# Windowed attention and a squared-relu feed-forward layer: the second chunk's steps run beside the first's, all in three products of split halves, with relu, square, scaling and splitting for two steps at once

## The chip, the cores and the metric

The kernel runs on one core of a Trainium2 chip. The metric is the device time of one execution in microseconds (us). The core's engines are TensorE (PE in the profile; PEld is its load of stationary operands), VectorE (DVE), ScalarE (ACT), GpSimd (POOL) and SyncE (SP), which issues all of this kernel's DMAs.

## The reference, cut to what matters

B, H, S, D = 4, 8, 768, 64; the feed-forward layer has 512 inputs, 2048 hidden units and 512 outputs. All is float32.

```
k_sum = k.reshape(B, H, 24, 32, D).max(axis=3)
v_sum = v.reshape(B, H, 24, 32, D).mean(axis=3)
scores_l = scale * q @ k.T, kept where |i - j| < 16, else -1e9
scores_s = scale * q @ k_sum.T + log(32)
a = softmax(concat[scores_l, scores_s])
x = a @ concat[v, v_sum]                  # 3072 tokens x 512
h = x @ w_in                              # 512 x 2048
g = s * relu(h)**2 + b
out = g @ w_out                           # 2048 x 512
```

## The kernel before, in words

The 3072 tokens are worked on in 12 chunks of 256 (three for each batch entry), the heads in four pairs p. The hidden layer is cut into 16 slices of 128 units, the steps f. For a chunk c the kernel makes x (attention) and then, for each step, the hidden layer (`hidden`, tile ph, 128 units x 256 tokens), relu and square (`activate`, tile r), scaling (`scaled`, tile g) and the projection (`project`), which adds all steps into two tiles po of 128 tokens x 512.

*Attention.* For a pair: `scores` (tile ps, L310 and L313), `masked` on VectorE (L328, tile pr), `exps` on ScalarE (L341), `normalize` on VectorE (L348, L349, L351), `transposes` on TensorE (L360, tile pt), `turned` (a copy, pT), `values` (tile pav, L394 and L396), `attended` (x, tile xh) and `attended_low` (its lower half, xl, L412). `k_max` makes block maxima of k (L165), `fill_k` and `fill_v` put maxima and means into the loaded tiles on GpSimd (L267, L272). The first chunk makes its products with maxima and means apart (`scores_of_maxima`, `mean_of_rows`, `values_of_means`).

*Weights and halves.* Weights come as 64-bit numbers in two words and are loaded by 32 DMAs (`load_weights`), scaled on ScalarE (L131, L132), and put together on VectorE (L140, L141, tile wf). A product of float32 accuracy is made in one of two ways. Plain: one fp32 product with wf. Split: wf is divided into an upper half wh (`upper_weights`, a cast to fp32r on either engine, L228 or L230) and a lower half wl (`lower_weights`, VectorE, L153), x into xh and xl, g into gh and gl (`upper_rows`, `lower_rows`, L483), and three fp32r products are added: lower by upper, upper by lower, upper by upper (L446 and L498).

*Which steps are plain.* The first chunk's steps 0 to 7 are plain (L429, and L498 with wf); its steps 8 to 15 (the table THREE) and all steps of the other chunks are split. The first chunk's x is kept whole and split later, in one piece (`first_upper`, `first_lower`, L421). The second chunk goes through the steps in another order, 8 to 15 first (SECOND). Relu, square, scaling and the split of g are one instruction for each step, 128 x 256.

*Storage.* SBUF: eight slots of 128 x 2048 hold raw weights, pairs of wh, and at the start k, q and rows of v; a ring of 17 holds wf and wl. PSUM has eight banks: two each for po, ph and ps, one for pt and one for pav.

*Order.* The program is recorded in a fixed order. From the start through most of the second chunk and the third chunk's attention it is a table written out by hand, FIRST_ORDER: a letter names a function (S scores, M masked, E exps, N normalize, T transposes, C turned, V values, X attended, y attended_low, H and Y hidden, J activate, G scaled, a and b upper and lower rows, P project, h and l upper and lower weights, A and D scaling and conversion of weights, i, o and w loads of weights, u and x loads of q with k and of v, W fillers), digits give chunk, pair or step, and stars choose the engine. Each engine works through its part of it in order. What is left follows from rules with steps (`then`): four hidden steps of a chunk, then the four projections of the group before, and so on. This loop begins with the third chunk's first four hidden steps.

Of the kernel before, what the change touches and what calls it, by code (L numbers as in the profile page):

```python
# [44 lines left out]
def windowed_attention_then_relu2_ffn(ctx, tc, qk, vwin, kt, vt, kq, vrow, wp, out):  # L45
# [33 lines left out]
    ones = const.tile([P, P], F32, name="ones")  # L79
    nc.vector.memset(ones, 1.0)  # L80
# [23 lines left out]

    THREE = (8, 9, 10, 11, 12, 13, 14, 15)
    SECOND = THREE + tuple(f for f in range(NF) if f not in THREE)


    def steps(c):
        return SECOND if c == 1 else tuple(range(NF))  # L110

# [31 lines left out]
    def upper_weights(f, other=False):  # L143
        j = SECOND.index(f)
# [38 lines left out]
    def v_mean(bi, g):  # L183
        if g == 0:
            vsum[bi] = p2.tile([P, H, D], F32, name="vsum", bufs=1)
        vs = p2.tile([96, D], F32, name="vmean")
# [17 lines left out]
    def keep_warm(n):  # L204

        t = ps_po.tile([P, DM], F32, name="warm", tag="po")
        for _ in range(n):
            nc.tensor.matmul(t[:, :P], ones, ones, start=True, stop=True)
# [80 lines left out]
    def scores(c, p, j):  # L289
        q, kw = qk_t[c, p]  # L290
        if j == 0:
# [5 lines left out]
            elif p == 2:  # L297
# [47 lines left out]
    def normalize(c, p):  # L345
# [7 lines left out]
    def transposes(c, p):  # L353
        pr = pr_of.pop((c, p))
        if together(c) and p % 2:
# [22 lines left out]
    def values(c, p):  # L378
# [3 lines left out]
        elif c < 2 or p % 2 == 0:  # L382
            if together(c) and p:
# [31 lines left out]
    def first_upper(other=False):  # L415
        xt["first"] = slot(F32R, "x0h")[:, 48 : 48 + NKC * T].rearrange("p (k t) -> p k t", t=T)
        copy(other, xt["first"], xt[0])

    def first_lower():
        xl["first"] = p2.tile([P, NKC, T], F32R, name="x0l", tag="xl")  # L420
        nc.vector.tensor_tensor(xl["first"], xt[0], xt["first"].bitcast(F32), ALU.subtract)  # L421


    ph_of, ph_both, r_of, gg, po = {}, {}, {}, {}, {}

    def hidden_part(f, kc):
        if kc == 0:
            ph_of[0, f] = ps_h.tile([P, 2, T], F32, name="ph", tag="ph")[:, f % 2]
        nc.tensor.matmul(  # L429
            ph_of[0, f], w_f[f][:, kc * P : (kc + 1) * P], xt[0][:, kc], start=(kc == 0), stop=(kc == NKC - 1)  # L430
        )

    def hidden(c, f):
        if c == 0 and f not in THREE:
            for kc in range(NKC):
                hidden_part(f, kc)
            return
        xh, xlow = (xt["first"], xl["first"]) if c == 0 else (xt[c], xl[c])
        if c < 2 or f % 2 == 0:
            ph_both[0] = ps_h.tile([P, 2, T], F32, name="ph", tag="ph")  # L440
        ph = ph_of[c, f] = ph_both[0][:, f % 2]
        terms = [
            (w[f], x, kc) for w, x in ((w_l, xh), (w_h, xlow), (w_h, xh)) for kc in range(NKC)
# [18 lines left out]
    def scaled(c, f, other=False):  # L462
        if c == 0 and f not in THREE:
            g = p2.tile([P, T], F32, name="g0", tag="gh", bufs=8)
        else:
            g = p2.tile([P, T], F32, name="g")
        gg[c, f] = (g,)
        r = r_of.pop((c, f))
        if other == 2:
            nc.scalar.activation(g, r, AF.Identity, bias=b_col, scale=s_col)  # L470
        else:
            (nc.vector if other else nc.gpsimd).tensor_scalar(g, r, s_col, b_col, ALU.mult, ALU.add)  # L472

    def upper_rows(c, f, other=False):
        (g,) = gg[c, f]
        gh = p2.tile([P, T], F32R, name="gh", tag="gh", bufs=8)
        copy(not other, gh, g)
        gg[c, f] = g, gh

    def lower_rows(c, f):  # L480
        g, gh = gg[c, f]
        gl = p2.tile([P, T], F32R, name="gl", bufs=7)
        nc.vector.tensor_tensor(gl, g, gh.bitcast(F32), ALU.subtract)  # L483
        gg[c, f] = gh, gl

    def project(c, f):
        if f == steps(c)[0]:
            for t in range(T // P):
                po[t] = ps_po.tile([P, DM], F32, name="po", tag="po")
        g = gg.pop((c, f))  # L490
        if c == 0 and f not in THREE:
            terms = [(g[0], w_f[f])]
        else:
            gh, gl = g
            terms = [(gl, w_h[f]), (gh, w_l[f]), (gh, w_h[f])]
        for t in range(T // P):
            for n, (a, w) in enumerate(terms):
                nc.tensor.matmul(  # L498
                    po[t], a[:, t * P : (t + 1) * P], w[:, 512:],
                    start=(f == steps(c)[0] and n == 0), stop=(f == steps(c)[-1] and n == len(terms) - 1),  # L500
                )

    def evict(c, t, other=False):
        o = stage.tile([P, DM], F32, name="o", tag="stage")
        copy(other, o, po[t])
# [35 lines left out]
    )  # L541
    def of(fn, *more):
# [8 lines left out]
        "F": mean_done, "t": fill_v, "X": attended, "y": attended_low, "Xh": first_upper, "Xl": first_lower,  # L551
# [55 lines left out]
    for j, f in enumerate(SECOND):  # L607
        then(NF - 3 + j, SPLIT, upper_weights, f)
        then(NF - 3 + j, SPLIT, lower_weights, f)
    for i in range(NF, NC * NF):  # L610
        c, j = divmod(i, NF)
        f = steps(c)[j]
# [68 lines left out]
```

## Time and profile before

| | |
|---|---|
| Time of the kernel, median of 3 runs | 630.0 us (629.89 to 630.21) |
| The profiled execution, its own time | 630.13 us |
| Its span, first to last instruction | 628.4 us |
| TensorE busy, share of the span | 616.9 us, 98% |
| VectorE busy | 324.2 us, 52% |
| ScalarE busy | 311.8 us, 50% |
| GpSimd busy | 178.4 us, 28% |
| Read from memory, written | 59.09 MB, 6.29 MB |

Engine busy times are sums over the span; the end of a matmul is modelled, so a busy TensorE is not one at its peak. Instructions of one engine overlap a little: what one costs in a row of them is the time from its start to the next one's start, shorter than its listed duration. Rows of the timeline give start, duration, engine, line, operation, output and input, shapes, and in brackets the idle time ahead with what ended it.

### The profile page before, as it was taken

To read this page: it belongs to the slowest core of one execution; us is meant where nothing else is said; L and a number is where in the kernel's file an instruction comes from. 1 tells how busy PE (TensorE), PEld (TensorE's weight loads), DVE (VectorE), ACT (ScalarE), POOL (GpSimd) and SP (SyncE) were. 2 spreads that over 40 slices of the span, in tenths; PEclk is the share of its full clock that TensorE was granted. 3 is DMA by queue.
4 is the path that set the end of the run, shared out by engine and by line. 5 is a ranking of instruction groups with operands and counts; after the bars stand their busy time and mean duration, and the time that the engine had idled before them with its cause. 6 is when DMAs were issued, how large, how long until landed. Compare 5 with 4: busy or idle time off the path is not lost.

```text
span 628.4 us, 14231 instructions
## 1 busy us (share of the span) xinstructions
PE 616.9 (98%) x5330; PEld 549.9 (88%) x5330; DVE 324.2 (52%) x1033; ACT 311.8 (50%) x927; POOL 178.4 (28%) x342
## 2 busy tenths in 40 slices
PE   6999999999999999999999999999999999999997
PEld 5766789989989998999899899998998999899896
DVE  6999989865354246345454235336435325523311
ACT  4999967463463364265245436436345336323321
POOL 3126213111611422322242321341151151232211
PEclk9999999999999999999999999999999999999999
DMA  8999413006205016103502211600620500200000
GB/s 340 414 418 417 196 47 120 4 16 198 75 14 181 2 45 223 50 19 102 167 19 101 82 43 49 226 19 0 221 65 2 181 0 20 85 1 2 35 0 34
DMA packets 26997, 66.45 MB, mean 106 GB/s; under 512 B 3824, under 2 KB 3824, under 8 KB 26928
## 3 DMA queue, kind: packets, MB, share of 16 engines
q1 hardware_dynamic: 26928, 65.54, 29.2%
q8 instruction: 42, 0.69, 0.4%
q14 instruction: 27, 0.22, 0.1%
HBM read 59.09 MB, written 6.29 MB: 104 GB/s over the span
## 4 chain that ended last, share of the span: by engine, by line
PE 87%; DMA 4%; DVE 3%; ACT 1%; issue 1%; DVEq 0%; SPq 0%; ACTq 0%
PE po L498 40%; PE ph L446 39%; PE pav L396 3%; DMA wraw<-in_wp_dram 3%; PE pt L360 3%; PE ps L310 3%; DMA qk<-in_qk_dram 1%; DVE wf L141 1%; DVE wf L140 1%; ACT wraw L131 0%; ACT wraw L132 0%; DVE wl L153 0%; DVE x0l L421 0%; DVE r L458 0%; DVE pr L328 0%
## 5 line engine op out<-in xcount | busy, mean ns | idle before, releaser
L472 POOL TENSOR_SCALAR g<-r,sb_col 128x256 f32<-128x256 f32 x180 | 113.5, 632 | 394.8 <-ACT r L460 267.0
L228 DVE CAST gh<-g 128x256 fp32r<-128x256 f32 x173 | 51.6, 299 | 244.4 <-POOL g L472 242.9
L454 ACT ACTIVATE r<-ph 128x256 f32<-128x256 f32 x186 | 70.2, 378 | 207.0 <-PE ph L446 197.7
L498 PE MATMUL po<-wh,gl 128*128 128x512 f32 x368 | 147.3, 400 | 0.9 <-DVE gl L483 0.9
L498 PE MATMUL po<-wh,gh 128*128 128x512 f32 x368 | 144.8, 393 | 0.0
L498 PE MATMUL po<-wl,gh 128*128 128x512 f32 x368 | 143.8, 391 | 0.0
L446 PE MATMUL ph<-xh,wl 128*128 128x256 f32 x704 | 109.4, 277 | 0.0
L446 PE MATMUL ph<-xl,wh 128*128 128x256 f32 x704 | 108.6, 276 | 0.0
L446 PE MATMUL ph<-xh,wh 128*128 128x256 f32 x704 | 108.5, 276 | 0.0
L483 DVE TENSOR_TENSOR gl<-g,gh 128x256 fp32r<-128x256 f32 x184 | 85.5, 466 | 32.8 <-PE po L498 16.5
L446 PEld LDWEIGHTS ph<-xh,wl 128*128 128x128 f32 x704 | 97.0, 188 | 4.4 <-issue 0.2
L446 PEld LDWEIGHTS ph<-xl,wh 128*128 128x128 f32 x704 | 93.4, 188 | 0.0
L446 PEld LDWEIGHTS ph<-xh,wh 128*128 128x128 f32 x704 | 92.9, 188 | 0.0
L341 ACT ACTIVATE pr<-pr,mn 128x120 f32<-128x120 f32 x176 | 66.9, 382 | 34.8 <-DVE mn L328 34.7
L498 PEld LDWEIGHTS po<-wh,gl 128*128 128x128 f32 x368 | 69.1, 188 | 16.2 <-DVE gl L483 2.0
L498 PEld LDWEIGHTS po<-wh,gh 128*128 128x128 f32 x368 | 69.1, 188 | 14.9
L498 PEld LDWEIGHTS po<-wl,gh 128*128 128x128 f32 x368 | 69.2, 188 | 13.5
L460 ACT ACTIVATE r<-r 128x256 f32<-128x256 f32 x183 | 76.5, 418 | 6.5 <-DVE r L456 0.8
L272 POOL COPY vw<-vsum 24x256 f32<-24x256 f32 x88 | 46.2, 553 | 19.9 <-PE po L498 10.8
L230 ACT COPY o<-po 128x512 f32<-128x512 f32 x23 | 13.5, 589 | 42.0 <-PE po L498 40.9
L341 ACT ACTIVATION_READ_ACCUMULATOR pr<-pr,mn 128x1 f32 x176 | 33.0, 187 | 0.0
L351 DVE TENSOR_TENSOR pr<-pr,rs 128x480 f32<-128x480 f32 x48 | 31.8, 661 | 1.7
(95 smaller groups left out, 556.5 us busy)
## 6 DMA issues: line engine op xcount, KB each, us to landing
wraw<-in_wp_dram SPq DMA_DIRECT2D x32, 512.0 KB
qk<-in_qk_dram SPq DMA_DIRECT2D x44, 369.0 KB
vw<-in_vwin_dram SPq DMA_DIRECT2D x48, 256.0 KB
out_dram<-o SPq DMA_DIRECT2D x24, 256.0 KB
kraw<-in_kt_dram SPq DMA_DIRECT2D x12, 384.0 KB
vraw<-in_vt_dram SPq DMA_DIRECT2D x12, 252.0 KB
kq<-in_kq_dram SPq DMA_DIRECT2D x4, 512.0 KB
vraw<-in_vt_dram SPq DMA_DIRECT2D x6, 264.0 KB
```

The source lines that it names most:

```text
L228: nc.vector.tensor_copy(out_, in_)
L272: nc.gpsimd.tensor_copy(vw_t[c, p][WIN:KR, e], vsum[bi][WIN : WIN + NB, 2 * p + e, :].unsqueeze(1).to_broadcast([NB, NSUB, D]),)
L310: nc.tensor.matmul(o, qi, kw[r, i, :], start=True, stop=True)
L341: nc.scalar.activation(pr, pr, AF.Exp, bias=mn_of[c, p][:, n : n + 1], scale=-1.0, accum_out=sm_of[c, p][:, n : n + 1])
L351: nc.vector.tensor_tensor(pr, pr, rs.unsqueeze(2).to_broadcast([P, 4, KR]), ALU.mult)
L360: nc.tensor.transpose(pt_of[c, p][:KR, n * P : (n + 1) * P], pr[:, n, :], ident)
L446: nc.tensor.matmul(ph, w[:, kc * P : (kc + 1) * P], x[:, kc], start=(n == 0), stop=(n == len(terms) - 1))
L454: nc.scalar.activation(r, ph, AF.Relu)
L460: nc.scalar.activation(r, r, AF.Square)
L472: (nc.vector if other else nc.gpsimd).tensor_scalar(g, r, s_col, b_col, ALU.mult, ALU.add)
L483: nc.vector.tensor_tensor(gl, g, gh.bitcast(F32), ALU.subtract)
L498: nc.tensor.matmul(po[t], a[:, t * P : (t + 1) * P], w[:, 512:], start=(f == steps(c)[0] and n == 0), stop=(f == steps(c)[-1] and n == len ...
```

## The change

The first chunk's plain steps go: all steps of all chunks are split. THREE, SECOND, `first_upper` and `first_lower` are removed; the first chunk's x is made as xh and xl at once, pair by pair, like the others. The table FIRST_ORDER is new: the second chunk's attention stands ahead of nearly all hidden steps, and the steps of the first and the second chunk follow each other, step by step, from step 0 on (H1.0, H1.1, H0.2, H1.2, H0.3 and so on); all weights are split as they come. The first chunk's steps 0 and 1 are made by `hidden_part` as before, in pieces of 128 inputs between the attention's parts, now with three products for each piece.

Relu, square, scaling and the two halves of g are one instruction for two steps, 128 x 512; scaling is made in place. The second chunk's output is added up in the PSUM banks of pt and pav, so both po banks are left to the first; the third chunk's transposes and values use the two banks of ps, and all its scores too. In the first chunks `normalize` adds its 1e-9 on GpSimd instead of VectorE. The fillers multiply the identity instead of a tile of ones, 12 of them instead of 9.

```
-    THREE = (8, 9, 10, 11, 12, 13, 14, 15)
-    SECOND = THREE + tuple(f for f in range(NF) if f not in THREE)
...
-            elif p == 2:
+            elif p == 2 and c > 2:
                 both = [ps_h.tile([P, 2 * T], F32, name="ps", tag="ph")[:, : 4 * KR] for _ in range(2)]
...
-        nc.vector.tensor_scalar(rs, sm_of.pop((c, p)), 1e-9, None, ALU.add)
+        (nc.gpsimd if other else nc.vector).tensor_scalar(rs, sm_of.pop((c, p)), 1e-9, None, ALU.add)
...
-        if together(c) and p % 2:
+        if c == 2:
+            pt_of[c, p] = ps_s.tile([P, 4 * P], F32, name="pt", tag="ps")
+        elif together(c) and p % 2:
...
-            if together(c) and p:
+            if c == 2:
+                o_of[c, p] = ps_s.tile([P, 2 * T], F32, name="pav", tag="ps")
+            elif together(c) and p:
...
-            xt[c] = p2.tile([P, NKC, T], F32R if c else F32, name="xh", tag="xh")
+            xt[c] = p2.tile([P, NKC, T], F32R, name="xh", tag="xh")
...
+    def first_products(ph, w, x, low, kc, first, last):
+        k = slice(kc * P, (kc + 1) * P)
+        for n, (a, b) in enumerate(((w_l[w], x), (w_h[w], low), (w_h[w], x))):
+            nc.tensor.matmul(ph, a[:, k], b[:, kc], start=(first and n == 0), stop=(last and n == 2))
...
     def hidden_part(f, kc):
...
-        nc.tensor.matmul(
-            ph_of[0, f], w_f[f][:, kc * P : (kc + 1) * P], xt[0][:, kc], start=(kc == 0), stop=(kc == NKC - 1)
-        )
+        ph = ph_of[0, f // 2][:, (f % 2) * T : (f % 2 + 1) * T]
+        first_products(ph, f, xt[0], xl[0], kc, kc == 0, kc == NKC - 1)
...
-    def activate(c, f, other=0):
-        r_of[c, f] = r = p2.tile([P, T], F32, name="r")
-        ph = ph_of.pop((c, f))
+    def activate(c, q, other=0):
+        gg[c, q] = r = p2.tile([P, 2 * T], F32, name="r")
+        ph = ph_of.pop((c, q))
...
+    def scaled(c, q, other=False):
+        g = gg[c, q]
+        if other == 2:
+            nc.scalar.activation(g, g, AF.Identity, bias=b_col, scale=s_col)
         else:
+            (nc.vector if other else nc.gpsimd).tensor_scalar(g, g, s_col, b_col, ALU.mult, ALU.add)
...
-        gh = p2.tile([P, T], F32R, name="gh", tag="gh", bufs=8)
+        gh = p2.tile([P, 2 * T], F32R, name="gh", bufs=4)
...
-        gl = p2.tile([P, T], F32R, name="gl", bufs=7)
+        gl = p2.tile([P, 2 * T], F32R, name="gl", bufs=4)
...
-                po[t] = ps_po.tile([P, DM], F32, name="po", tag="po")
+                pool, tag = ((ps_t, "pt"), (ps_v, "pav"))[t] if c == 1 else (ps_po, "po")
+                po[c, t] = pool.tile([P, DM], F32, name="po", tag=tag)
...
-        if c == 0 and f not in THREE:
-            terms = [(g[0], w_f[f])]
-        else:
-            gh, gl = g
-            terms = [(gl, w_h[f]), (gh, w_l[f]), (gh, w_h[f])]
+        gh, gl = (g[:, (f % 2) * T : (f % 2 + 1) * T] for g in gg[c, f // 2])
+        terms = [(gl, w_h[f]), (gh, w_l[f]), (gh, w_h[f])]
...
-        "q1 S0.1.0 S0.1.1 q0 W1 K0.1 S0.0.0 S0.0.1 Z1 K0.0 Z0 M0.1.0 q2 q3 u1.0 M0.0.0 r2 M0.0.1 W8 r0 E0.1.0 "
+        "q1 S0.1.0 S0.1.1 K0.1 Z1 q0 S0.0.0 S0.0.1 q2 W1 K0.0 Z0 M0.1.0 q3 M0.1.1 M0.0.0 M0.0.1 E0.1.0 i0 K0.2 "
```

More of the change, by code (lines that the diff above doesn't have):

```diff
@@ L102, in windowed_attention_then_relu2_ffn @@
         )
-    THREE = (8, 9, 10, 11, 12, 13, 14, 15)
-    SECOND = THREE + tuple(f for f in range(NF) if f not in THREE)
-    def steps(c):
-        return SECOND if c == 1 else tuple(range(NF))
     w_raw, w_f, w_h, w_l, held = {}, {}, {}, {}, {}
@@ L207, in keep_warm @@
         for _ in range(n):
-            nc.tensor.matmul(t[:, :P], ones, ones, start=True, stop=True)
+            nc.tensor.matmul(t[:, :P], ident, ident, start=True, stop=True)
     pm = []
@@ L343, in exps, with normalize @@
             )
-    def normalize(c, p):
+    def normalize(c, p, other=False):
         mn_of.pop((c, p))
         rs = p2.tile([P, 4], F32, name="rs")
-        nc.vector.tensor_scalar(rs, sm_of.pop((c, p)), 1e-9, None, ALU.add)
+        (nc.gpsimd if other else nc.vector).tensor_scalar(rs, sm_of.pop((c, p)), 1e-9, None, ALU.add)
         nc.vector.reciprocal(rs, rs)
@@ L412, in attended_low, with hidden_pair @@
         nc.vector.tensor_tensor(xl[c][:, kcs], o, xt[c][:, kcs].bitcast(F32), ALU.subtract)
[L415 to L424, printed above, removed]
+    ph_of, gg, po = {}, {}, {}
+    def first_products(ph, w, x, low, kc, first, last):
+        k = slice(kc * P, (kc + 1) * P)
+        for n, (a, b) in enumerate(((w_l[w], x), (w_h[w], low), (w_h[w], x))):
+            nc.tensor.matmul(ph, a[:, k], b[:, kc], start=(first and n == 0), stop=(last and n == 2))
+    def hidden_pair(c, f):
+        if f % 2 == 0:
+            ph_of[c, f // 2] = ps_h.tile([P, 2 * T], F32, name="ph", tag="ph")
+        return ph_of[c, f // 2][:, (f % 2) * T : (f % 2 + 1) * T]
     def hidden_part(f, kc):
         if kc == 0:
-            ph_of[0, f] = ps_h.tile([P, 2, T], F32, name="ph", tag="ph")[:, f % 2]
-        nc.tensor.matmul(
-            ph_of[0, f], w_f[f][:, kc * P : (kc + 1) * P], xt[0][:, kc], start=(kc == 0), stop=(kc == NKC - 1)
-        )
+            hidden_pair(0, f)
+        ph = ph_of[0, f // 2][:, (f % 2) * T : (f % 2 + 1) * T]
+        first_products(ph, f, xt[0], xl[0], kc, kc == 0, kc == NKC - 1)
     def hidden(c, f):
-        if c == 0 and f not in THREE:
[L435 to L441, printed above, removed]
+        ph = hidden_pair(c, f)
         terms = [
-            (w[f], x, kc) for w, x in ((w_l, xh), (w_h, xlow), (w_h, xh)) for kc in range(NKC)
+            (w[f], x, kc) for w, x in ((w_l, xt[c]), (w_h, xl[c]), (w_h, xt[c])) for kc in range(NKC)
         ]
@@ L460, in activate, with upper_rows, lower_rows @@
             nc.scalar.activation(r, r, AF.Square)
[L462 to L476 removed]
+    def scaled(c, q, other=False):
+        g = gg[c, q]
+        if other == 2:
+            nc.scalar.activation(g, g, AF.Identity, bias=b_col, scale=s_col)
+        else:
+            (nc.vector if other else nc.gpsimd).tensor_scalar(g, g, s_col, b_col, ALU.mult, ALU.add)
+    def upper_rows(c, q, other=False):
+        g = gg[c, q]
+        gh = p2.tile([P, 2 * T], F32R, name="gh", bufs=4)
         copy(not other, gh, g)
[L478 to L482 removed]
+        gg[c, q] = g, gh
+    def lower_rows(c, q):
+        g, gh = gg[c, q]
+        gl = p2.tile([P, 2 * T], F32R, name="gl", bufs=4)
         nc.vector.tensor_tensor(gl, g, gh.bitcast(F32), ALU.subtract)
[L484 removed]
+        gg[c, q] = gh, gl
     def project(c, f):
[L487 removed]
+        if f == 0:
             for t in range(T // P):
[L489 to L495 removed]
+                pool, tag = ((ps_t, "pt"), (ps_v, "pav"))[t] if c == 1 else (ps_po, "po")
+                po[c, t] = pool.tile([P, DM], F32, name="po", tag=tag)
+        gh, gl = (g[:, (f % 2) * T : (f % 2 + 1) * T] for g in gg[c, f // 2])
+        terms = [(gl, w_h[f]), (gh, w_l[f]), (gh, w_h[f])]
         for t in range(T // P):
@@ L498, in project @@
                 nc.tensor.matmul(
-                    po[t], a[:, t * P : (t + 1) * P], w[:, 512:],
-                    start=(f == steps(c)[0] and n == 0), stop=(f == steps(c)[-1] and n == len(terms) - 1),
+                    po[c, t], a[:, t * P : (t + 1) * P], w[:, 512:],
+                    start=(f == 0 and n == 0), stop=(f == NF - 1 and n == len(terms) - 1),
                 )
@@ L504, in evict @@
         o = stage.tile([P, DM], F32, name="o", tag="stage")
-        copy(other, o, po[t])
+        copy(other, o, po[c, t])
         bi, ci = place(c)
@@ L606, in windowed_attention_then_relu2_ffn @@
                 then(xa, ATT, attended_low, c, p)
-    for j, f in enumerate(SECOND):
-        then(NF - 3 + j, SPLIT, upper_weights, f)
-        then(NF - 3 + j, SPLIT, lower_weights, f)
+    for f in range(NF):
+        then(NF - 3 + f, SPLIT, upper_weights, f)
+        then(NF - 3 + f, SPLIT, lower_weights, f)
     for i in range(NF, NC * NF):
-        c, j = divmod(i, NF)
-        f = steps(c)[j]
+        c, f = divmod(i, NF)
         then(i - i % 4, HID, hidden, c, f)
-        for stage_of in (activate, scaled, upper_rows, lower_rows):
-            then(i, CHAIN, stage_of, c, f)
+        if f % 2:
+            for stage_of in (activate, scaled, upper_rows, lower_rows):
+                then(i, CHAIN, stage_of, c, f // 2)
         then((i + 4) | 3, PROJ, project, c, f)
-        if j == NF - 1:
+        if f == NF - 1:
             for t in range(T // P):
```

8 lines of the change are left out of this document (3 added, 5 removed), and 46 rows, old and new, of the table FIRST_ORDER.

## The prediction, made before the changed kernel ran

> **What bounds the kernel now.** I read the page first, then TensorE's chain of waits, then the busy times of four stages, then the engines' timelines in the first 120 us. The chain, followed in order of time, is nearly all TensorE from 77 us on:
>
> ```profile
> 104.57 1.39 PE ph L446 x12
> 105.95 1.37 PE po L498 x6
> 108.72 0.44 PE pt L360 x4
> 123.83 2.02 PE pav L396 x64
> 125.85 1.80 PE ps L310 x64
> 130.60 5.47 PE ph L446 x48
> 613.83 11.00 PE po L498 x48
> ```
>
> So one step (a slice of 128 hidden units for one chunk of 256 tokens) costs TensorE 1.39 us for the hidden layer and 1.37 us for the projection, 2.76 us in three products. At 130.60 us the third chunk's hidden steps begin, and from there both kernels run the same planned loop. The four stages, with busy time and instructions of PE, PEld, DVE, ACT and POOL, clock, DMA share and GB/s:
>
> ```profile
> 0.00:21.23 21.23, 15.65 (x322) 12.95 (x322) 14.97 (x65) 12.92 (x50) 6.37 (x32) 1.00 0.92 359
> 21.23:77.85 56.62, 54.56 (x390) 39.38 (x387) 53.54 (x100) 53.55 (x105) 20.53 (x26) 1.00 0.89 361
> 77.85:130.60 52.75, 52.50 (x488) 47.50 (x489) 46.32 (x139) 33.44 (x97) 10.82 (x21) 1.00 0.18 56
> 130.60:180.22 49.62, 49.62 (x434) 45.30 (x434) 24.46 (x87) 22.60 (x77) 15.02 (x28) 1.00 0.30 91
> ```
>
> From 130.60 us on TensorE is never idle while VectorE is busy 24.46 of 49.62 us: cheaper work on the other engines buys nothing there. Up to 77.85 us VectorE and ScalarE are both 95% busy, and TensorE is covered only because the first chunk's steps 0 to 7 use plain fp32, which needs no halves. The result therefore hangs on one number: when the third chunk's first hidden step starts. Everything behind that point should last as long as before.
>
> **The change part by part.** *Plain fp32 becomes three products.* TensorE's timeline has the fp32 steps (each instruction leaves two records):
>
> ```profile
> 42.82 3.60 PE L498 MATMUL po<-wf,g 128*128 128x512 f32 x8
> 46.26 3.62 PE L429 MATMUL ph<-xh,wf 128*128 128x256 f32 x16
> 49.71 3.60 PE L498 MATMUL po<-wf,g 128*128 128x512 f32 x8
> ```
>
> Two projections take 46.26 - 42.82 = 3.44 us, two hidden steps 3.45 us, so a step is 3.445 us against 2.76 us in three products. Eight steps save 8 x 0.685 = 5.5 us of TensorE's work. That is the whole gain on TensorE; the rest of the change decides how much of it is lost to waiting.
>
> *The halves are needed earlier.* Before, TensorE starts the first hidden step between the first chunk's attention products:
>
> ```order
> L394 MATMUL pav<-vn,vw 64x64 x8
> L429 MATMUL ph<-xh,wf 128x256
> L373 MATMUL pav<-vn,vsum 64x64 x8
> L394 MATMUL pav<-vn,vw 64x64 x8
> L373 MATMUL pav<-vn,vsum 64x64 x8
> L429 MATMUL ph<-xh,wf 128x256 x7
> L310 MATMUL ps<-qk 64x120 x8
> ```
>
> Now, at the same place, it stands behind two transposes and a score of the second chunk (first row), and takes xl and wl:
>
> ```order
> L301 MATMUL ps<-qk 64x120 x8
> L415 MATMUL ph<-xh,wl 128x256
> L415 MATMUL ph<-xl,wh 128x256
> L415 MATMUL ph<-xh,wh 128x256
> L353 MATMUL pt<-ident,pr 120x128 x4
> L391 MATMUL pav<-pT,vw 64x64 x8
> L389 MATMUL pav<-vn,vw 64x64 x8
> ```
>
> The second chunk's attention has moved ahead of the hidden steps. On VectorE, before, the first x was split in one piece while weights were converted:
>
> ```order
> L228 COPY xh<-pav 128x256
> L228 CAST x0h<-xh 128x1024
> L140 TENSOR_SCALAR wf<-wraw 128x1024
> L141 ISA wf<-wraw,wf 128x2048
> L458 TENSOR_TENSOR r<-r 128x256 x2
> ```
>
> Now the last lower parts of both chunks' x and the halves of steps 1 and 2 (wl, wh) stand together, and the second chunk's first full hidden step needs all rows up to the last xl here:
>
> ```order
> L407 TENSOR_TENSOR xl<-pav,xh 128x256 x2
> L144 TENSOR_TENSOR wl<-wf,wh 128x1024
> L219 CAST xh<-pav 128x256
> L407 TENSOR_TENSOR xl<-pav,xh 128x256
> L131 TENSOR_SCALAR wf<-wraw 128x1024
> L132 ISA wf<-wraw,wf 128x2048
> L407 TENSOR_TENSOR xl<-pav,xh 128x256
> L219 CAST wh<-wf 128x1024
> L144 TENSOR_TENSOR wl<-wf,wh 128x1024
> ```
>
> I add up VectorE's rows ahead of such a place, priced by start-to-start times of its timeline:
>
> ```profile
> 15.08 0.18 DVE L349 RECIPROCAL rs<-rs 128x4 f32<-128x4 f32 x1
> 15.29 0.66 DVE L351 TENSOR_TENSOR pr<-pr,rs 128x480 f32<-128x480 f32 x1
> 15.87 0.27 DVE L328 CUSTOM_DVE_ANT_0 pr<-ps,mask_mid 128x120 f32<-128x120 f32 x1
> 16.07 0.28 DVE L328 CUSTOM_DVE_ANT_0 pr<-ps,mask_mid 128x120 f32<-128x120 f32 x1
> 37.06 0.69 DVE L140 TENSOR_SCALAR wf<-wraw 128x1024 uint32<-128x1024 uint32 x1
> 37.88 1.23 DVE L141 CUSTOM_DVE_ANT_0 wf<-wraw,wf 128x2048 uint16<-128x2048 uint16 x1
> 39.02 0.68 DVE L228 COPY pT<-pt 120x512 f32<-120x512 f32 x1
> 39.62 0.41 DVE L456 TENSOR_SCALAR r<-ph 128x256 f32<-128x256 f32 x1
> 71.47 0.32 DVE L228 CAST gh<-g 128x256 fp32r<-128x256 f32 x1
> 71.83 0.42 DVE L483 TENSOR_TENSOR gl<-g,gh 128x256 fp32r<-128x256 f32 x1
> 72.17 1.22 DVE L153 TENSOR_TENSOR wl<-wf,wh 128x1024 fp32r<-128x1024 f32 x1
> 73.31 0.69 DVE L140 TENSOR_SCALAR wf<-wraw 128x1024 uint32<-128x1024 uint32 x1
> 75.43 0.42 DVE L412 TENSOR_TENSOR xl<-pav,xh 128x256 fp32r<-128x256 f32 x1
> 75.76 0.68 DVE L228 CAST wh<-wf 128x1024 fp32r<-128x1024 f32 x1
> 76.48 1.23 DVE L153 TENSOR_TENSOR wl<-wf,wh 128x1024 fp32r<-128x1024 f32 x1
> 99.08 0.95 DVE L165 TENSOR_REDUCE ksum<-kraw 128x24 f32<-128x768 f32 x1
> 99.94 0.29 DVE L228 CAST gh<-g 128x256 fp32r<-128x256 f32 x1
> ```
>
> Prices: a mask 0.20, a normalization 0.21 + 0.58, a maximum 0.86, a conversion 0.82 + 1.14 (in halves about 1.23 each), wl 1.14, wh 0.72, xl 0.33, gl 0.34. The 512-wide forms do not occur: gl lies between 0.34 (256 wide) and 1.14 (wl, the same operation 1024 wide), so 0.61 as an estimate; gh between 0.30 and 0.72, so 0.45. If a wide form cost two narrow ones the sum below would rise by about 1.5 us.
>
> In the new order, ahead of and with the lower half of step 10, VectorE does 13 steps' conversions (26.7 us, steps 0 and 1 in halves), 11 wl (12.4), 5 wh (3.7), 46 masks (9.2), 8 normalizations (6.3), 5 maxima (4.3), 8 xl and 3 xh (4.0), one pT (0.6), 8 gl, 4 gh and three other wide operations (8.6): 75.8 us, by the unrounded gaps 76.0. The same sum up to the last xl of the fence above is 30.8 us.
>
> What such a sum lacks is VectorE's offset: its late start, its waits and stretched rows. In the old order the sums ahead of these three rows, and of the wl at 76.48, are 18.8, 75.3, 104.8 and 67.9 us:
>
> ```profile
> 25.17 0.69 DVE L228 CAST x0h<-xh 128x1024 fp32r<-128x1024 f32 x1
> 85.11 1.22 DVE L153 TENSOR_TENSOR wl<-wf,wh 128x1024 fp32r<-128x1024 f32 x1
> 117.80 1.22 DVE L153 TENSOR_TENSOR wl<-wf,wh 128x1024 fp32r<-128x1024 f32 x1
> ```
>
> The offset was thus 6.4 us at 25 us, 8.6 at 76, 9.8 at 85 (there VectorE waits for TensorE, not the reverse) and 13.0 at 118. So the second chunk's first full hidden step may start at 30.8 + 6.4 = 37.2 us. From there to the hidden step 10 of the second chunk TensorE has 18 hidden steps, 14 projections and two scores, 44.8 us, and VectorE 76.0 - 30.8 = 45.2 us: they run neck and neck and VectorE's drift sets the pace. Behind it VectorE has 18.9 us to the last wl, TensorE 30.5 us before it uses that: no more waiting is due. I take an offset of 9.0 us, nearest the row at 76.48 with its drift carried on: step 10 starts at 76.0 + 9.0 = 85.0 us. TensorE then has 12 hidden steps (16.7), 14 projections (19.2), four transposes (1.8), values (2.0) and scores (1.8) to the third chunk's first hidden step: 41.5 us, so that starts at 126.5 us against 130.60: 4.1 us earlier. Put otherwise: 5.5 us less work, 1.4 us more waiting.
>
> *What goes with it.* **Pairs**: relu, square, scaling, gh and gl of two steps in one instruction save under 0.1 us each in VectorE's sums, already counted; in the loop TensorE hides them. Their chain is longer for a pair, but a projection stands one group of four (5.5 us) behind its hidden steps, and at the end 11.00 us of projections cover it: nothing. **The add of 1e-9 on GpSimd**: eight adds of 0.2 us leave VectorE; its reciprocal, and all splits queued behind it, now wait for GpSimd, where fills stand in front:
>
> ```profile
> 37.28 2.09 POOL L272 COPY vw<-vsum 24x256 f32<-24x256 f32 x2 [4.42 <-DMA vw<-in_vwin_dram]
> ```
>
> The order places the fills a few us ahead, so I take nothing; if the cover fails for the two normalizations behind a fill, 2.1 us each. **PSUM**: the second chunk's output accumulates in the banks of pt and pav, so the third chunk's transposes and values share the two ps buffers with its scores. TensorE reaches them more than 10 us after the masks that free them; nothing, or up to 2 us of round trips. **Weights on the queue**: the 32 loads are the same, but the ones of step 2 on stand on SP behind value loads that wait for a buffer of the first chunk's values (about 23 us). Step 2 is first needed by ScalarE at 33 us: hidden, and 2 us of dry queue otherwise. The ones fillers become 12 instead of 9, in waits.
>
> The profiled execution took 630.13 us, 0.13 above the median of 630.0, and its span is 628.4. 630.13 - 4.1 = **626.0 us**. By the offsets: 6.4 us gives 123.9 for the start and 623.4 us; 13.0 us gives 130.5 and 630.0 us.
>
> **Rivals.** *The order holds better than I think*: no drift, 623.4 us. For it: GpSimd's copies and fills, which stretch VectorE's rows, are fewer. Against: ScalarE is as full as VectorE. Chance 0.14.
>
> *Drift as in the later stretch*: VectorE waits for ScalarE's scaling as it did after 85 us; the offset reaches 13 and the gain is gone, 630.0 us. For it: ScalarE's share of 53.55 in 56.62 us leaves no room, and both work in turn on each weight. Chance 0.14.
>
> *Slower: hand-offs in the attention.* Both chunks' attention, eight units, must now be through before full hidden steps begin, each going TensorE, ScalarE, TensorE, VectorE. Such hand-offs cost ScalarE this in the old start:
>
> ```profile
> 11.94 0.59 ACT L230 COPY pT<-pt 120x512 f32<-120x512 f32 x1 [1.20 <-PE pt L360]
> 13.22 0.40 ACT L341 ACTIVATE pr<-pr 128x120 f32<-128x120 f32 x1 [0.69 <-DVE pr L328]
> ```
>
> If VectorE stands 0.8 us in each of the eight, its offset is 9.0 + 6.4 = 15.4 and the loop starts at 132.9: 632.4 us. It decides from an offset of 13.1 us on. Against it: the order keeps conversions between the units. Chance 0.12.
>
> *TensorE goes cold.* The fillers at the start ran slowly:
>
> ```profile
> 7.47 2.88 PE L208 MATMUL warm<-ones 128*128 128x128 f32 x16
> ```
>
> That is 0.18 us for 128 columns, where L429's records above took 0.216 for 256, so one such start lost 16 x (0.18 - 0.108) = 1.2 us, though the clock is given as 1.00. In the new order TensorE has only 20 us of work in its first 37. VectorE's pace leaves it 85.0 - 37.2 - 44.8 = 3.0 us, so one or two cold starts are absorbed and three cost 0.6 us: 626.6 us, chance 0.04. The Trainium skill ("TensorE: Matmul & The Clock Gate", What's actually happening) says that the array falls to half rate after an idle window of about 3.4 us and recovers after a busy one; by that the stretch ahead of 37 us would cost about 1.7 us per restart, an estimate. The filler row agrees in kind, the clock column does not show it.
>
> **How the numbers follow.** The forecast (offset 7.5 to 11.5, 624.5 to 628.6 us) has 0.56. Faster by over 0.2% (1.3 us, about what a measurement of this kernel can tell) are the forecast, the better case and the cold one: 0.74; the drift case is the same: 0.14; slower: 0.12. The range runs from 622.8, just below the case without drift, to 631.0, above the drift case with half the price of a late fill; it leaves out about 2 in 10.
>
> **What would show it.** In the new profile: no fp32 products of hidden or projection; the first x4 hidden of the second chunk near 37 us; VectorE over 90% busy to 80 us; the first hidden group of the third chunk at 126.5 us, followed by the same 49.62 us period. I am wrong if TensorE waits inside the loop, if VectorE has idle time before 80 us waiting for GpSimd or ScalarE, or if the loop starts after 130.6 us.

## The result and the profile after

| | before | after |
|---|---|---|
| Time, median (range) | 630.11 us (629.89 to 630.42, 4 runs) | 625.1 us (624.04 to 625.4, 4 runs) |
| Ratio, 95% interval | | 0.9917, 0.99 to 0.9934 |
| Profiled execution, its span | 630.13, 628.4 us | 624.84, 622.7 us |
| VectorE, ScalarE, GpSimd busy | 324.2, 311.8, 178.4 us | 292.2, 294.2, 135.5 us |

The changed kernel is 5.0 us faster. The chain of waits after, in order of time (start, us, what):

```profile
28.71 7.19 DMA wraw<-in_wp_dram
35.98 1.17 ACT wraw L122
...
40.78 1.66 PE ph L434 x12
...
82.28 2.75 PE ph L434 x24
...
122.86 1.58 PE po L478 x6
```

The next row, from the same view of the whole execution, is the third chunk's first hidden group, with two that follow it:

```profile
124.44 5.66 PE ph L434 x48
130.10 5.51 PE po L478 x24
135.61 5.65 PE ph L434 x48
```

The group starts at 124.44 us where it started at 130.60: 6.16 us earlier (4.1 were forecast). Busy times of the stages after, the last one a period of the loop (PE, PEld, DVE, ACT, POOL, clock, DMA share, GB/s):

```profile
0.00:21.20 21.20, 15.34 (x276) 12.19 (x276) 15.00 (x67) 14.55 (x56) 8.56 (x38) 1.00 0.93 360
21.20:36.30 15.10, 14.41 (x276) 12.02 (x271) 14.46 (x44) 13.84 (x40) 6.46 (x14) 1.00 1.00 368
36.30:82.28 45.98, 45.75 (x336) 41.29 (x335) 44.09 (x83) 45.10 (x68) 4.89 (x6) 1.00 0.83 316
82.28:124.44 42.16, 42.16 (x374) 37.57 (x374) 33.81 (x67) 27.12 (x66) 8.04 (x16) 1.00 0.19 68
164.96:214.58 49.62, 49.62 (x434) 45.32 (x436) 17.40 (x63) 20.21 (x56) 11.53 (x20) 1.00 0.19 63
```

Three things are to be seen. The period is 49.62 us as before. From 36.30 us on TensorE has next to no idle time, so that it has taken over from VectorE and ScalarE as the engine whose work is the path. And between 36.30 and 82.28 us all three stand close together: 45.75, 45.10 and 44.09 of 45.98 us.

The account closes: start of the loop -6.16; from there to the span's end 498.26 against 497.80 us, +0.46, most of it in the groups of 5.66 and 5.65 us; outside the span 2.14 against 1.73, +0.41. Together -5.29 = 624.84 - 630.13.

### The profile page after: what moved, and what is told of

It reads as the page before. It is cut to its first block, busy times and chain, and to the rows that moved or that the text cites. A ratio compares the mean times of both kernels' runs of the same rounds, so it can differ in the third digit from the quotient of the medians.

```text
span 622.7 us, 13558 instructions
## 1 busy us (share of the span) xinstructions
PE 612.3 (98%) x5384; PEld 553.7 (89%) x5384; DVE 292.2 (47%) x838; ACT 294.2 (47%) x748; POOL 135.5 (22%) x257
## 4 chain that ended last, share of the span: by engine, by line
PE 93%; ACT 3%; DMA 2%; DVE 1%; issue 0%; SPq 0%; DVEq 0%; ACTq 0%
PE po L478 43%; PE ph L434 41%; PE pav L391 3%; PE pt L353 3%; PE ps L301 3%; ACT pr L332 1%; DMA wraw<-in_wp_dram 1%; DMA kq<-in_kq_dram 1%; DVE pr L342 0%; ACT wraw L122 0%; ACT wraw L123 0%; DVE ksum L156 0%; ACT vsum L221 0%; ACT r L442 0%; ACT r L453 0%
## 5 line engine op out<-in xcount | busy, mean ns | idle before, releaser
L219 DVE CAST gh<-r 128x512 fp32r<-128x512 f32 x88 | 37.7, 428 | 278.0 <-POOL r L455 269.1
L455 POOL TENSOR_SCALAR r<-r,sb_col 128x512 f32<-128x512 f32 x85 | 67.9, 799 | 408.2 <-ACT r L448 308.9
L442 ACT ACTIVATE r<-ph 128x512 f32<-128x512 f32 x93 | 55.8, 600 | 191.4 <-PE ph L434 178.7
L434 PE MATMUL ph<-xh,wl 128*128 128x256 f32 x760 | 118.8, 279 | 0.2 <-ACT r L442 0.2
L434 PE MATMUL ph<-xl,wh 128*128 128x256 f32 x760 | 117.5, 277 | 0.0
L434 PE MATMUL ph<-xh,wh 128*128 128x256 f32 x760 | 117.4, 277 | 0.0
L434 PEld LDWEIGHTS ph<-xh,wl 128*128 128x128 f32 x760 | 104.6, 188 | 5.6 <-ACT r L442 0.7
L466 DVE TENSOR_TENSOR gl<-r,gh 128x512 fp32r<-128x512 f32 x96 | 67.9, 708 | 4.1 <-ACT gh L221 1.3
L448 ACT ACTIVATE r<-r 128x512 f32<-128x512 f32 x92 | 58.2, 632 | 5.7 <-DVE r L444 2.9
L221 ACT COPY pT<-pt 120x512 f32<-120x512 f32 x44 | 23.9, 585 | 30.0 <-PE pt L353 29.8
```

The source lines that it names most:

```text
L219: nc.vector.tensor_copy(out_, in_)
L221: nc.scalar.copy(out_, in_)
L434: nc.tensor.matmul(ph, w[:, kc * P : (kc + 1) * P], x[:, kc], start=(n == 0), stop=(n == len(terms) - 1))
L442: nc.scalar.activation(r, ph, AF.Relu)
L448: nc.scalar.activation(r, r, AF.Square)
L455: (nc.vector if other else nc.gpsimd).tensor_scalar(g, g, s_col, b_col, ALU.mult, ALU.add)
```

## The experiments

**Theory**: from 36.3 us on TensorE's own work is the path, so the 5.5 us of cheaper products come out whole, as long as VectorE and ScalarE keep up. **Rivals**: VectorE's pace is the path (the forecast); the gain comes from the wide instructions for pairs; the arithmetic alone brings it; the fillers and the smaller moves do.

| Run | median (range), us | third chunk's first group |
|---|---|---|
| changed kernel again (base) | 625.24 (624.73 to 625.5) | 124.73 |
| six steps plain | 627.94 (627.83 to 629.29) | 127.88 |
| lighter lower halves, steps 2 to 10 | 624.51 (623.82 to 625.52) | 124.65 |
| lighter lower halves, steps 0 and 1 | 624.02 (623.87 to 624.14) | 124.14 |
| pairs undone on all engines | 627.84 (627.74 to 628.05) | 128.28 |
| pairs undone on ScalarE | 625.92 (625.29 to 627.04) | 125.74 |
| pairs undone on VectorE | 624.79 (624.38 to 626.22) | 125.11 |
| adds on VectorE | 625.23 (624.86 to 625.66) | 125.91 |
| no fillers | 625.35 (624.01 to 626.89) | 126.11 |
| step 0's lower half on GpSimd | 625.63 (625.45 to 626.3) | 125.61 |
| kernel before, emulated products | 630.23 (629.84 to 630.93) | 130.31 |
| the same, grouped | 630.38 (629.92 to 631.21) | 130.79 |

The kernel before beside them had 630.17 to 630.43 us. The last column is of the one profiled execution of each.

**The base.**

> The changed kernel once more, unchanged, as the base for the three runs beside it and for small differences of the earlier ones: 624.0 to 625.4 us, the range of its first runs. In the first profile the third chunk's first two hidden groups took 5.66 and 5.65 us where later ones take 5.46. If that belongs to this kernel's order, it shows again at the same place; if it is something that comes and goes on the chip, it shows elsewhere or not at all.

625.24 us; both hidden groups at the loop's start take the usual 5.46 and 5.47 us. The longer groups of the first profile don't come from this kernel's order: the run without fillers has two of them (5.66 us), the run with pairs undone on ScalarE has one, the other runs on the changed kernel have none.

**Whose work is the path: more for TensorE.**

```
     def hidden(c, f):
+        if c == 0 and 2 <= f <= 7:
+            for kc in range(NKC): matmul(ph, w_h[f] as F32, xt[c] as F32)
+            return
     def project(c, f):
+        if c == 0 and 2 <= f <= 7: terms = [(gh as F32, w_h[f] as F32)]
```

> The changed kernel with the first chunk's steps 2 to 7 as one fp32 product each, of the upper halves alone (the lower halves are left out of these steps' sums); all other instructions and their order stay. TensorE has 6 x 0.685 = 4.1 us more work, all of it ahead of the second chunk's step 10. If TensorE's own work sets the pace from 36.3 us on (theory), all of it shows: 625.1 + 4.1 = 629.2 us, and VectorE and ScalarE get idle time. If VectorE's pace sets it, as the prediction had it, with 3.0 us of waits in TensorE that take the first of it: 625.1 + 1.1 = 626.2 us. If the fp32 steps were not what the change saves: 625.1.

2.7 us slower in time, 3.15 in the start of the loop: much nearer to 4.1 than to 1.1. TensorE's stretch up to the second chunk's step 10:

```profile
36.30:85.42 49.12, 49.12 (x299) 39.87 (x297) 44.82 (x84) 45.57 (x70) 4.74 (x6) 1.00 0.77 299
```

In TensorE's timeline of the changed kernel the same step starts at 82.12 us, so it comes 3.3 us later here. Its second row of four products comes 3.7 us later (86.29 against 82.59 us), since the row behind the last fp32 products lasts longer (0.87 us to the next start, against 0.47). VectorE and ScalarE do the same work as there (44.82 and 45.57 us) and have 2.4 and 2.7 us more idle time. Of the 4.1 us TensorE's waits can have taken the 0.23 us that it idled there before, not 3.0; where the rest stays between this step and the end is not shown.

The run also says something on the new order. With six of the eight steps plain again the kernel is still 2.25 us faster than the kernel before beside it (630.19 us), and the two steps that stay split are worth 2 x 0.685 = 1.4 us by the prediction's price. By this estimate some 0.9 us comes from the other changes together.

**Whose work is the path: less for VectorE.**

```
     def lower_weights(f):
-        nc.vector.tensor_tensor(w_l[f], w_f.pop(f), w_h[f], subtract)
+        if 2 <= f <= 10: nc.vector.tensor_copy(w_l[f], w_h[f])
```

> The changed kernel with the lower halves of the weights of steps 2 to 10 made by a plain cast instead of the subtraction (the output lacks those halves). VectorE has 9 x (1.14 - 0.60) = 4.9 us less work between 36.3 us and the second chunk's step 10; nothing else changes. Theory (TensorE sets the pace): nothing to win but the 0.2 to 0.7 us of TensorE's gaps and slow hand-overs there, 624.4 to 625.1 us. VectorE's pace, as in the prediction: 3 to 4.9 us less, 620.2 to 622.1.

```profile
36.27:81.77 45.50, 45.50 (x334) 41.55 (x333) 39.47 (x82) 43.83 (x67) 2.70 (x6) 1.00 0.80 306
```

VectorE is busy 39.47 us instead of 44.09, and step 10 comes 0.35 us earlier (81.77 against 82.12), though VectorE has 4.6 us less to do. The median is 0.7 us lower, with overlapping ranges. VectorE's pace was not the path there; the forecast's account of this stretch falls.

**The same ahead of 36 us.**

```
+        if f < 2: nc.vector.tensor_copy(w_l[f], w_h[f])
```

> The changed kernel with the lower halves of the weights of steps 0 and 1 as plain casts (the output lacks those halves): VectorE has 2 x 0.54 = 1.1 us less ahead of the last xl. The prediction puts the first full hidden step where VectorE's sum ends, so that this step and the end come 1.1 us earlier: 624.0 us. If TensorE's and ScalarE's hand-overs in the attention hold the first 36 us: no change, 624.9 to 625.3 us.

1.2 us faster in the median, as the first account said, but not in the way it said. (Measured against the kernel before beside each, the difference is 0.9 us, and the intervals of the two ratios, 0.9887 to 0.9917 and 0.9903 to 0.9929, overlap.) The first full hidden step stays at 36.30 us, since VectorE now waits for TensorE's values (first row, VectorE; second, TensorE):

```profile
33.07 0.42 DVE L223 CAST xh<-pav 128x256 fp32r<-128x256 f32 x1 [0.28 <-PE pav L395]
```
```profile
36.30 0.62 PE L438 MATMUL ph<-xh,wl 128*128 128x256 f32 x4
```

Its profiled execution is 0.6 us below the base's (624.14 against 624.73), nearly all of it gained behind 36.30 us (the base has that step at 36.33). So this run doesn't show a gain from VectorE's shorter work; where the 1.2 us come from stays open.

**Pairs.** All engines narrow:

```
     def activate(c, q, other=0):
+        for n in (slice(0, T), slice(T, 2 * T)):
+            relu of r[:, n]; then square of r[:, n]
     (scaled, upper_rows, lower_rows: the same loop)
```

> The changed kernel with relu, square, scaling and both halves of g as two instructions of 128x256 for each pair, in all chunks, in the same places. By the prediction the pairs are worth under 0.1 us each on VectorE, eight pairs ahead of step 10, and nothing in the loop: 625.1 to 626.6 us. A second account: ScalarE is 45.1 of 46.0 us busy between 36.3 and 82.3 us, and two narrow ones cost it 0.16 us more for a relu (x9), 0.20 for a square (x8), 0.39 for a scaling (x6) and 0.19 for an upper half (x4), 6.1 us, so ScalarE would become the bound: the loop starts 3 to 6 us later, 628 to 631 us, and its period stays at 49.62 us. If the pairs matter in the loop: longer than 49.62.

2.6 us slower, period unchanged: half of the change's gain would be gone. Then ScalarE alone, the loop around each operation, so that two relus stand side by side, then two squares:

> The changed kernel with two instructions of 128x256 for each pair on ScalarE alone (relu, square, scaling, upper half); VectorE and GpSimd keep one of 128x512. ScalarE gets up to 6.1 us more work between 36.3 and 82.3 us, VectorE none. If a full ScalarE is what made the run with all pairs undone 2.7 us slower: 627.2 to 627.8 us. If it was VectorE: 625.1 to 625.8 us.

0.7 us slower only. And VectorE alone:

> The changed kernel with two instructions of 128x256 for each pair on VectorE alone (lower halves, and upper halves, relu, square and scaling where VectorE makes them); ScalarE and GpSimd keep one of 128x512. With all engines narrow it was 2.7 us slower, with ScalarE alone 0.8. If the rest is VectorE's own: 627.0 to 627.5 us, with TensorE waiting for wl and gl. If it takes both engines, each waiting for the other: 625.1 to 625.8 us. The prediction priced a wide form at little less than two narrow ones, about 1.5 us in VectorE's sum up to step 10: 626.6 us.

No difference that can be told. So the width of VectorE's instructions costs nothing here, ScalarE's costs little, and what is left to tell the last two runs from the first is the order in which ScalarE's narrow instructions stand, or both engines narrow at once. ScalarE's timeline for the first pair, from its relu to the next pair's. After:

```profile
38.09 0.57 ACT L442 ACTIVATE r<-ph 128x512 f32<-128x512 f32 x1
38.70 0.63 ACT L448 ACTIVATE r<-r 128x512 f32<-128x512 f32 x1
39.43 0.82 ACT L453 ACTIVATE r<-r,sb_col 128x512 f32<-128x512 f32 x1
40.15 0.58 ACT L442 ACTIVATE r<-ph 128x512 f32<-128x512 f32 x1
```

Narrow on ScalarE, side by side:

```profile
37.97 0.62 ACT L444 ACTIVATE r<-ph 128x256 f32<-128x256 f32 x2
38.50 0.71 ACT L451 ACTIVATE r<-r 128x256 f32<-128x256 f32 x2
39.11 1.08 ACT L457 ACTIVATE r<-r,sb_col 128x256 f32<-128x256 f32 x2
```

Narrow on all engines, relu and square in turn:

```profile
37.62 0.41 ACT L443 ACTIVATE r<-ph 128x256 f32<-128x256 f32 x1
38.06 0.42 ACT L449 ACTIVATE r<-r 128x256 f32<-128x256 f32 x1
38.38 0.37 ACT L443 ACTIVATE r<-ph 128x256 f32<-128x256 f32 x1
38.78 0.42 ACT L449 ACTIVATE r<-r 128x256 f32<-128x256 f32 x1
39.10 1.08 ACT L455 ACTIVATE r<-r,sb_col 128x256 f32<-128x256 f32 x2
40.09 0.36 ACT L443 ACTIVATE r<-ph 128x256 f32<-128x256 f32 x1
```

The first pair takes 40.15 - 38.09 = 2.06 us wide, 2.13 side by side (the next relu starts at 40.10) and 40.09 - 37.62 = 2.47 in turn. A square that follows its own relu starts 0.03 us after that has ended (38.03, 38.06); an instruction that needs nothing of the one ahead starts 0.10 us before its end (39.20, 39.10). The Trainium skill ("ScalarE: Activation LUTs", What ACT_TABLE_LOAD costs) says that back-to-back activations overlap by about 93 ns; the rows agree for independent ones and not for dependent ones.

Relu and square alone, up to the next instruction, take 39.11 - 37.97 = 1.14 us side by side and 39.10 - 37.62 = 1.48 in turn. Seven pairs with both operations on ScalarE stand ahead of step 10, and in turn each takes 0.29 to 0.35 us longer, 2.2 us together. ScalarE had 45.98 - 45.10 = 0.9 us left there, and in turn it waits for nothing between 36 and 84 us. TensorE comes to step 10 at 82.12 us wide, at 83.21 side by side and at 84.19 in turn. From its first full hidden step up to there it idles 0.23, 0.55 and 1.78 us; the same 335 products take it 45.59, 46.44 and 46.10 us, a difference that the narrow instructions don't explain. So the alternation goes with 1.2 us of waiting ahead of step 10. Behind step 10, where the wide kernel's TensorE never idles, it waits 1.1 us in turn for VectorE's wl and gl, most of it here:

```profile
109.06 0.71 PE L434 MATMUL ph<-xh,wl 128*128 128x256 f32 x4 [0.81 <-DVE wl L144]
```

That the alternation is the main cause is argued from these rows and not shown: no run undid it alone, and none made GpSimd's scaling alone narrow. The 6.1 us that I had put down for narrow instructions were differences of listed durations, which hide the overlap; for the first pair the rows give 0.07 us.

**Arithmetic alone.** Two substitutes for three products in the old order:

```
-    matmul(ph, wf, x)                                  # fp32, 256 columns, for each of 4 kc
+    matmul(ph, ones, ones) fp32r; matmul(ph[:, :64], wf, x[:, :64]) fp32; matmul(ph, ones, ones) fp32r
```

> The kernel before, its order kept, with the time of three fp32r products in place of each plain fp32 product (a narrow fp32 product with the real operands, so that all waits stay, and two fp32r products of a constant tile at full width; the first chunk's plain steps are thereby left out of the result). TensorE has 8 x 0.685 = 5.5 us less work up to 77 us, VectorE and ScalarE the same work as before, 95% busy. Theory (the new order and the lighter ScalarE are needed to turn the saved work into time): TensorE waits instead, 628 to 630.1 us. Rival (the arithmetic alone does it): 630.1 - 5.5 = 624.6 us.

> As the run on the kernel before with emulated products, but with the narrow fp32 products of a step side by side instead of one between every two fp32r products, so that the kind changes twice in a step and not eight times. Now a hidden step should take about 1.4 us instead of 1.72 and a projection 1.37 instead of 1.72: some 4.7 us less TensorE work up to 57 us, waits and other engines as before. Theory (VectorE and ScalarE set the pace of the old order there): TensorE waits for wl and r instead, 628.8 to 630.2 us. Rival (the cheaper products alone bring the gain): 625 to 626 us.

Both equal the kernel before, but the runs don't answer the question: the substitute isn't cheap. In the grouped run:

```profile
45.78 0.28 PE L452 MATMUL ph<-ones 128*128 128x256 f32 x1
46.08 1.10 PE L448 MATMUL ph<-xh,wf 128*128 128x64 f32 x8
46.99 0.48 PE L452 MATMUL ph<-ones 128*128 128x256 f32 x2
```

The eight fp32 records take 46.99 - 46.08 = 0.91 us, 0.114 each, over half of the 0.216 that four times the columns take, and each change of kind adds more, so hidden steps saved nothing. TensorE's busy time between 21.2 and 77.85 us fell by 1.1 us only (53.46 against 54.59), and ahead of 21.2 us it rose by 1.0 (16.66 against 15.62). Whether cheaper products without the new order would have brought anything stays open.

**Small terms.** The adds of 1e-9 back on VectorE:

> The changed kernel with the add of 1e-9 in normalize on VectorE again. VectorE has eight more instructions of 0.2 us ahead of the last xl, 1.6 us in all, and waits no longer for GpSimd. VectorE's sum sets the first full hidden step (prediction): up to 626.7 us. Theory (VectorE has its work done in its waits for exps there, since reciprocal and add stand behind the same wait): 625.1 to 625.6 us. If the fills on GpSimd delay the adds now: faster than 625.1.

625.23 us, the same. The profiled execution shows the first full hidden step later:

```profile
37.20 0.62 PE L434 MATMUL ph<-xh,wl 128*128 128x256 f32 x4
```

That is 0.9 us of the 1.6, and the medians don't show it. The fillers away:

> The changed kernel without its 12 filler products. The rival of a cold TensorE would have its work of the first 20 us run slowly: 1.2 us for each stretch that starts cold, 626.3 us or more, and rows of attention products longer than 0.64 us for 16. If the fillers only fill waits for data: 624.5 to 625.4 us.

The median is the same, the range nearly four times as wide. In its profiled execution (626.47 us) TensorE is slow until 20 us. Here are rows of products with means (L208) and scores (L301) from the slow time and a row of scores behind it:

```profile
16.06 1.07 PE L208 MATMUL pm<-vn,mean 128*24 128x128 f32 x16
17.06 1.08 PE L301 MATMUL ps<-qk 64*64 64x120 f32 x16
18.07 1.07 PE L208 MATMUL pm<-vn,mean 128*24 128x128 f32 x16
...
22.37 0.64 PE L301 MATMUL ps<-qk 64*64 64x120 f32 x16
```

The changed kernel with its fillers has, in turn, the fillers themselves, the first fast row, and products with means:

```profile
7.69 3.10 PE L199 MATMUL warm<-ident 128*128 128x128 f32 x16
10.72 0.56 PE L304 MATMUL ps<-kq 64*64 64x96 f32 x16
...
16.27 0.64 PE L208 MATMUL pm<-vn,mean 128*24 128x128 f32 x16
```

Sixteen products with means take 1.00 us from start to start cold and 0.56 warm. The fillers run cold themselves and the array is fast right behind them. The clock column says 1.00 for both kernels there. The first full hidden step came at 37.37 instead of 36.33 us. The Trainium skill ("TensorE: Matmul & The Clock Gate", What's actually happening) says that the array starts at half rate, speeds up after about 3.4 us of sustained work, and counts in windows that run freely, so that the switch differs from execution to execution. The rows agree with the first (ratio 1.8). With fillers they agree with the second (3.0 us of fillers); without them TensorE works without a gap from 15.02 us on and is still slow at 19.07, which takes longer. The third would allow that and would fit the wide range, but no run shows it.

**A try at a better version.**

```
-    nc.vector.tensor_tensor(w_l[0], w_f.pop(0), w_h[0], subtract)
+    nc.gpsimd.tensor_tensor(w_l[0], w_f.pop(0), w_h[0], subtract)
```

> A try at a better version: the lower half of step 0's weights is subtracted on GpSimd (at 20.9 us, used at 26.1), so that VectorE has 1.14 us less ahead of the last xl and all results stay. If VectorE's sum sets the first full hidden step: 624.0 us. If the hand-overs of the attention hold it, as the first full hidden step at 36.30 us in the run with light early halves says: within 0.3 us of the changed kernel beside it. If GpSimd stretches VectorE's rows meanwhile or holds up the adds behind it: up to 1 us slower.

0.4 us slower than the base. GpSimd's and VectorE's timelines show the price:

```profile
20.62 2.37 POOL L145 TENSOR_TENSOR wl<-wf,wh 128x1024 fp32r<-128x1024 f32 x1 [0.96 <-DVE wh L220]
22.94 0.18 POOL L194 COPY sb_col<-qk 128x2 f32<-128x2 f32 x1
23.20 0.22 POOL L340 TENSOR_SCALAR rs<-sums 128x4 f32<-128x4 f32 x1
```
```profile
23.46 0.18 DVE L341 RECIPROCAL rs<-rs 128x4 f32<-128x4 f32 x1 [0.68 <-POOL rs L340]
```

The subtraction takes 2.37 us there against 1.22 on VectorE, the add of a normalization stands behind it, and VectorE waits for that add. The first full hidden step comes at 37.83 us. No version here with its result intact beats the changed kernel by more than the ranges overlap.

## Why the prediction was right, step by step

*The one number.* It said that all hangs on the start of the third chunk's hidden steps and that the rest lasts as long. Right: over the profiled executions, time less that start is 499.5 to 500.4 us in all kernels, before and after.

*Term 1, 5.5 us less TensorE work.* Right in size: six steps put back cost 3.3 to 3.7 of 4.1 us by step 10. Ahead of the loop TensorE was busy 122.7 us before (15.65 + 54.56 + 52.50) and 117.7 after (15.34 + 14.41 + 45.75 + 42.16), 5.05 us less. The loop starts 6.16 us earlier, so the other 1.1 us are waits that went, where the forecast had 1.4 us of waits added.

*The first full hidden step at 37.2 us.* It came at 36.30 us. VectorE's rows:

```profile
35.94 0.42 DVE L407 TENSOR_TENSOR xl<-pav,xh 128x256 fp32r<-128x256 f32 x1
...
41.22 0.69 DVE L466 TENSOR_TENSOR gl<-r,gh 128x512 fp32r<-128x512 f32 x1
41.82 1.22 DVE L144 TENSOR_TENSOR wl<-wf,wh 128x1024 fp32r<-128x1024 f32 x1
...
80.47 1.22 DVE L144 TENSOR_TENSOR wl<-wf,wh 128x1024 fp32r<-128x1024 f32 x1
```

With the last xl done at 35.94 + 0.33 = 36.27 and a sum of 30.8, the offset was 5.5 us and not 6.4. The estimate of 0.61 us for a wide gl met 0.60 (41.82 - 41.22). But VectorE's sum alone doesn't set this step, as the forecast had it: with lighter early halves the sum was shorter and the step stayed at 36.30, since VectorE then waited for TensorE's values.

*"They run neck and neck and VectorE's drift sets the pace", offset 9.0, step 10 at 85.0 us.* This step failed. The lower half of step 10 was done at 80.47 + 1.14 = 81.6 us, and with the sum of 76.0 the offset is 5.6 us: no drift between 36 and 81 us. TensorE came to step 10 at 82.28 us after 45.98 us for 44.8 us of work, and the runs with lighter lower halves and with plain steps show that its own work set that time. The 1.4 us of added waiting didn't come. I had carried over the drift of the old order, where VectorE waited for ScalarE and GpSimd seven times between 30 and 118 us, 3.4 us in all. That is half of the 6.6 us by which the offset had grown from 25 to 118 us; no run took the other half apart. In the new order its waits between 36 and 81.6 us are these (us in total, times, longest):

```profile
DVE r L446 <- ACT r L442: 0.5, 1, 0.5
DVE wf L132 <- ACT wraw L123: 0.4, 2, 0.3
```

ScalarE's results mostly stand ready there; no row of the old trace told that they would. The forecast's own case, an offset from 7.5 to 11.5, did not come. VectorE's idle time ahead of 80 us while it waited for ScalarE, one of its signs of being wrong, is there too, but small: 1.4 us in all.

*41.5 us from there to the loop.* It took 42.16 us: the first product after one of another kind is longer, as in the 1.58 us of six projections behind scores, which else take 1.37. With the 0.46 us in the loop and the 0.41 outside the span these took back a part of what the missing drift gave, so that 626.0 was 0.9 us off, though the offset was off by 3.4 us and step 10 came 2.7 us early. That the total came so near is in part luck.

*Pairs "nothing".* Right for the loop and for VectorE. In the start it held by the way they are written: ScalarE, which my sums left out, had 0.9 us of room up to step 10, and with all pairs undone, relu and square in turn, the kernel loses 2.6 us.

*Costed at nothing.* What TensorE waited for in the first 125 us after (us in total, times, longest):

```profile
PE ps L304 <- DMA kq<-in_kq_dram: 4.1, 1, 4.1
PE ps L301 <- DVE pr L319: 0.8, 1, 0.8
PE pt L353 <- ACT pT L221: 0.7, 2, 0.4
PE pav L366 <- ACT vsum L221: 0.5, 1, 0.5
PE pt L353 <- ACT vn L221: 0.2, 1, 0.2
PE ph L434 <- ACT r L442: 0.2, 1, 0.2
```

The list shows no wait for the PSUM that the third chunk's attention shares (the wait for ps at L301 is a score at 14 us), and none behind the adds on GpSimd; VectorE's waits in the same time don't name GpSimd either. The weights on the queue cost a little: the chain runs through the load of step 2's weights (28.71 us), for which ScalarE waited 0.34 us, and TensorE 0.23 us at 40.78 us for the relu behind it.

*Rivals.* No drift, which had a chance of 0.14, was the nearest: it gave a start of 123.9 us, and the offset stayed where it was at 36 us. The hand-offs in the attention did not cost the 6.4 us of their rival: TensorE waits for ScalarE's copies there for 1.4 us in all. The cold array is real, but with the fillers it was over by 10.7 us.

## What to carry to other kernels

Sum each engine's queue up to the point where the next engine needs it, and do so for every engine that is nearly full, not only for the fullest: here the one left out, ScalarE, was the one that an innocent rewrite overloaded. An offset measured in an old order belongs to that order: here its value before the drift was the better forecast. And price narrow against wide instructions by the distance from start to start in a real sequence, with the dependent neighbour beside it, not by listed durations.

## What the runs showed of the chip

A narrow activation that needs the one ahead starts 0.03 us after its end, an independent one 0.10 us before it (in the wide rows above a dependent one starts 0.04 and 0.10 us after it). An fp32 product with 64 columns takes 0.114 us a record, with 256 columns 0.216. In some stretches, of 3 to 16 us, four hidden products take 0.47 us instead of 0.454 (groups of 5.66 us instead of 5.46) with the clock column at 1.00. Some come and go: one was at the loop's start in the first profile and not in the base. Another stands in both, behind transposes at 105 us. What makes them is not shown. GpSimd's subtraction of 128x1024 takes 2.37 us, 1.94 times VectorE's 1.22.
